# Half-width array tiles for PV, the state term and k^T v, in one burst for two chunks, in a fused linear-attention and ELU-MLP kernel

## The chip, the cores and the metric

The kernel runs on one core of a Trainium2 chip. The metric is device time in microseconds (us); smaller is better. Seven runs of the kernel before gave a median of 221.62 us, from 220.46 to 222.16.

## What is computed

Two stages follow each other. The first is causal linear attention with a decay per head, for batch 4, 8 heads, 768 tokens and head size 64. The reference works through the sequence in blocks and carries a 64x64 state per batch and head:

```python
intra = np.einsum('bhic,bhjc->bhij', qb, kb) * Dmask[None]
intra = np.einsum('bhij,bhjd->bhid', intra, vb)
inter = np.einsum('bhid,bhde->bhie', qb * lam_pow[None], kv_state)
out[:, :, sl] = intra + inter
kv_state = lam_block * kv_state + np.einsum('bhsd,bhse->bhde', kb_dec, vb)
```

The second takes the attention output as 3072 tokens of 512 features, multiplies by `w_in` (512x2048), applies ELU, and multiplies by `w_out` (2048x512). Inputs and output are float32; the kernel computes with float16 operands and float32 accumulation.

## The kernel before

The kernel uses blocks of 128 tokens. A chunk g is one block of one batch: g = 4 * block + batch, so there are 24 chunks, and chunk g needs the state that chunk g - 4 left. Heads are handled in four pairs (hp), two heads (hh) to a pair. For a chunk the steps are, with the letters of the kernel's own program:

- T (lines 272 to 300): q and k are transposed. Chunks 0 to 7 do it on TensorE, with DVE (line 298) scaling q while it copies and ACT (line 299) copying k. Chunks 8 to 23 use transposing DMAs on SP's queue.
- S (line 302): k q^T, 8 matmuls with 64 contracted rows, the two heads of a pair on the upper and lower half of the array. E (line 315) multiplies by the decay mask on DVE and makes `pp`.
- P (line 324): for each head pair two PV matmuls and, from chunk 4 on, one state-term matmul, all accumulated in one 128x128 block of the PSUM tile psO. So that one head's product fills only its own half, v lies in a tile `vz` with 64 zero columns between heads: head 0 takes [v0, 0], head 1 takes [0, v1] as 128-column weights. Then psO is copied to `xt`, the input of the MLP, by ACT (line 349, chunks 0 to 7) or by DVE with q's scale (line 351).
- U (line 374): k^T v for the state, 4 matmuls of 128x128 (line 381), of which only the two diagonal 64x64 blocks are used; DVE adds them into the state (line 392) after POOL has decayed the old one (`stt`, line 364). POOL also makes the decayed k, `kd` (line 175).
- 1 (line 418, matmuls on line 427): 8 or 16 matmuls by `w_in` into psH, of which there are two buffers; ACT does exp and relu (lines 433 and 434). `flush` at the next unit does the ELU combination `g` on DVE (line 410). Chunks 0 to 3 go singly, later ones in pairs with 256 columns.
- 2 (line 439, matmuls on line 449): four matmuls of 512 columns by `w_out` into psM, and after the fourth such unit of a chunk a copy (line 464) and a store.

The order is written out by hand. `OPEN` (line 51) lists the units of roughly the first 82 us in the order in which every engine's queue gets them; a number with colons is an MLP unit (1:chunk:part or 2:chunk:part). After it a loop (lines 530 to 557) puts the attention steps of each later pair of chunks at fixed places ahead of the pair's first MLP unit (`AT`, line 61): S 8 units ahead, P 5 and 4, U 3 and 2. `TAGS` names the PSUM bank of each product, eight banks in all. `POOL_ORDER` (line 45) is the order of POOL's queue: loads that convert to float16 on the way (q, k, v with a chunk number; i and o for parts of `w_in` and `w_out`), the index constants (iota), `kd` (d) and `stt` (m). An m waits for a token M in `OPEN`. Two tiles don't come over POOL: `RAW` (line 49) loads q of chunk 0 on SP's queue and k of chunk 0 on ACT's queue as float32, and DVE and ACT convert them (lines 128 and 130).

The zero columns are written once: DVE sets those of chunks 0 to 2 at the start (line 201), ACT those of chunk 3 (line 203) and those of the four pair buffers (line 468). The state tiles, which are block-diagonal, are zeroed too: one of each batch by DVE (line 206), the other by ACT (line 471).

Of the kernel before, what the change touches and what calls it, by code (L numbers as in the profile page):

```python
# [15 lines left out]
def kernel(  # L16
# [11 lines left out]
    nc = tc.nc  # L28
# [17 lines left out]
        "k2 v1 q2 iota q1 k1 i1 v0 i0 o1 v2 i3 o0 i2 q3 o2 k3 d0 d2 i4 d1 i5 o3 o7 v3 o5 o4 d3 "  # L46
        "i6 i7 o6 k4 q4 k10 k6 d4 v4 v8 q6 d5 q10 m4 v10 m5 m6 v6 d6 k8 q8 d7 m7"
    )
    RAW = "q0 k0"
    FIRST = "q0:0 c0 k0:1 c1 c2"  # L50
    OPEN = (
        "v3:1 Z2 Z0 z2 Z1 V0 z0 T0 z3 z1 V1 T1 S0 T2 S1 P0 S2 P1 1:0:0 P2 U0 1:1:0 1:2:0 2:0:0 "
        "1:0:1 2:1:0 M 1:1:1 T3 2:2:0 1:2:1 1:0:2 S3 2:1:1 1:1:2 2:2:1 2:0:1 P3 1:2:2 1:3:1 "
        "2:1:2 U1 1:3:0 2:0:2 1:1:3 Z3 U2 2:2:2 1:0:3 1:2:3 T5 2:1:3 M T4 2:0:3 2:2:3 1:3:2 "
        "S4:5 2:3:0 1:3:3 P4 E5 V3 2:3:1 U4 2:3:2 P5 U5 1:4:1 2:3:3 U3 M 1:4:0 W8 M W9 T6 "
        "1:4:2 T7 1:4:7 V2 S6:7 1:4:3 2:4:0 1:4:4 E7 2:4:1 1:4:5 P6 1:4:6 U7 P7 U6 2:4:2 1:6:0 "
        "1:6:1 2:4:3 S8:9 1:6:2 2:5:2 1:6:4 W10 2:5:1 W11 2:5:3 E9 1:6:3 2:6:0 2:5:0 U8 P8 "
        "1:6:5 1:6:6 2:6:1 P9 U9 1:6:7 2:6:2"
    )
    LAGU = 7  # L60
    AT = {"W": -13, "T": -9, "S": -8, "P": -5, "U": -3}
    TAGS = {
        "S0": "M0 M1", "S1": "C D", "S2": "A B", "S3": "A B",
        "P0": "H", "P1": "M0", "P2": "C", "P3": "A",
        "U0": "A", "U1": "A", "U2": "A", "U3": "B",
        "T0": "A B", "T1": "H H", "T2": "A B", "T3": "D", "T4": "A", "T5": "B", "T6": "A", "T7": "C",
        "T8": "B", "T9": "D", "M2": "C", "M3": "M0", "M4": "M1", "M5": "M0",
    }

# [17 lines left out]
    PB = 4  # L87
    vz1 = [cpool.tile([128, 1, 2 * H, 64], FP16, name=f"vz1_{i}") for i in range(4)]
    vz2 = [cpool.tile([128, 2, 2 * H, 64], FP16, name=f"vz2_{i}") for i in range(PB)]
# [6 lines left out]
    def emit_load(w, g0):  # L96
        n = size_of[g0]
        c, b = divmod(g0, B)
        x = {"q": q, "k": k, "v": v}[w]
        src = x[b : b + n, :, c * L : (c + 1) * L].rearrange("b h p d -> p (b h) d")  # L100
        if w == "v":
            t = vz1[g0] if n == 1 else vz2[(g0 - 4) // 2 % PB]
            assert g0 < 4 + 2 * PB or {f"{w}{g0 - i}" for w in "PU" for i in (7, 8)} <= seen
            vg[g0] = t
            dst = t[:, :, 0::2, :]
        else:
            t = asb.tile([128, n, H, 64], FP16, tag=f"{w}n{n}", name=f"{w}n{g0}", bufs=4)
            (qg if w == "q" else kg)[g0] = t
            dst = t[:]
        nc.gpsimd.dma_start(out=dst.rearrange("p b h d -> p (b h) d"), in_=src)  # L110
# [88 lines left out]
    def zero_v1(i, eng=0):  # L199
        if eng == 0:  # L200
            nc.vector.memset(vz1[i][:, :, 1::2, :], 0.0)
        else:
            nc.scalar.memzero(vz1[i][:, :, 1::2, :])

# [4 lines left out]
    for i in range(3):  # L209
        zero_v1(i)  # L210
# [52 lines left out]
    def default_tags(g):  # L263
        a, b = ("A", "B") if g % 2 == 0 else ("C", "D")
        for w, t in (("S", f"{a} {b}"), ("P", a), ("U", b), ("M", f"M{(g + 1) % 2}")):
            TAGS.setdefault(f"{w}{g}", t)
# [47 lines left out]

    def att_E(g):
        pts = psS.pop(g)
        for hh in range(2):
            P = asb.tile([128, NHP, 128], FP16, tag="pp", name=f"pp{g}_{hh}", bufs=6)
            nc.vector.tensor_tensor(  # L319
                out=P[:], in0=pts[hh][:], in1=mask[:, hh::2, :], op=ALU.mult  # L320
            )
            Pt[(g, hh)] = P

    def att_P(g):
        cb, b = divmod(g, B)
        vt = of(vg, g)
        qt, _ = qkT[g]
        po = bank(f"P{g}", 0, [128, NHP, 128], FP32, f"psO{g}")
        for hp in range(NHP):
            for hh in range(2):  # L330
                b0 = 4 * hp + hh
                nc.tensor.matmul(  # L332
                    po[:, hp, :], lhsT=vt[:, b0 : b0 + 2, :], rhs=Pt[(g, hh)][:, hp, :],
                    start=(hh == 0), stop=(hh == 1 and cb == 0), skip_group_check=True,
                )
            if cb > 0:
                nc.tensor.matmul(  # L337
                    po[:, hp, :], lhsT=st[b][cb % 2][:, hp, :], rhs=qt[:, hp, :],
                    start=False, stop=True, skip_group_check=True,
                )  # L340
        g0 = GFIRST[g]
        n = GSIZE[g0]
        if g0 not in xg:
            xg[g0] = asb.tile(
                [128, NHP, n * 128], FP16, tag=f"xt{n}", name=f"xt{g0}", bufs=4 if n == 1 else 2
            )
        dst = xg[g0][:, :, (g - g0) * 128 : (g - g0 + 1) * 128]
        if g < GPE:
            nc.scalar.copy(out=dst, in_=po[:])
        else:  # L350
            nc.vector.tensor_tensor(out=dst, in0=po[:], in1=qs[:], op=ALU.mult)  # L351
# [3 lines left out]
    def att_M(g):  # L355
        cb, b = divmod(g, B)
        if cb == NCB - 1:
            return
        assert f"U{g - B}" in seen
        old = st[b][cb % 2]  # L360
        for hh in range(2):
            r = slice(hh * 64, (hh + 1) * 64)
            tmp = asb.tile([128, NHP, 64], FP32, tag="stt", name=f"stt{g}_{hh}", bufs=8)
            nc.gpsimd.tensor_tensor(  # L364
                out=tmp[r], in0=old[r, :, r],
                in1=upp[r].unsqueeze(2).broadcast_to([64, NHP, 64]), op=ALU.mult,
            )
            stt[(g, hh)] = tmp
# [5 lines left out]
    def att_U(g):  # L374
        cb, b = divmod(g, B)
        if cb == NCB - 1:
            return
        vt = of(vg, g)
        pu = bank(f"U{g}", 0, [128, NHP, 128], FP32, f"psU{g}")
        for hp in range(NHP):  # L380
            nc.tensor.matmul(  # L381
                pu[:, hp, :].rearrange("p (h e) -> p h e", h=2),
                lhsT=kds[g][:, 2 * hp : 2 * hp + 2, :],
                rhs=vt[:, 4 * hp : 4 * hp + 3 : 2, :], start=True, stop=True,
            )
        new = st[b][(cb + 1) % 2]
        for hh in range(2):
            r = slice(hh * 64, (hh + 1) * 64)
            if cb == 0:
                nc.vector.tensor_copy(new[r, :, r], pu[r, :, r])  # L390
            else:
                nc.vector.tensor_tensor(  # L392
                    out=new[r, :, r], in0=stt.pop((g, hh))[r], in1=pu[r, :, r], op=ALU.add
                )

# [9 lines left out]
    def flush():  # L405
        while pending:
# [7 lines left out]
            for f in range(FB // n):  # L414
                for c in range(n):
                    gts[(g0 + c, j * (FB // n) + f)] = g[:, f, c, :]

    def mm1(g0, j):
# [3 lines left out]
        assert {f"P{g0 + i}" for i in range(n)} <= seen  # L422
        pH = ps.tile([128, FB * 128], FP32, tag="psH", bufs=2, name=f"psH{g0}_{j}")
# [43 lines left out]
    def zero_v(i):  # L467
        nc.scalar.memzero(vz2[i][:, :, 1::2, :])

# [12 lines left out]
    seen = {"v0", "v1", "v2"}  # L482

    def ready(t):

        if t[0] in "12M":
            return
        g = int(t[1:].split(":")[0])
        if t[0] == "P":
            assert (g < B or f"U{g - B}" in seen) and (  # L490
                (f"v{g}" if g < 3 else "v3" if g == 3 else f"V{(g - 4) // 2 % PB}") in seen
            )
# [4 lines left out]
        seen.add(t.split(":")[0])  # L497

    def run(t):
        ready(t)  # L500
        a = t[1:].replace(":", " ").split()
        a = [int(x) for x in a]
        if t[0] == "S":
            att_S(a[0])
            if len(a) == 1:
                att_E(a[0])
            else:
                att_S(a[1])
                att_E(a[0])
        else:  # L510
            {"T": att_T_pe, "E": att_E, "P": att_P, "U": att_U, "1": mm1, "2": mm2,
             "V": zero_v, "Z": zero_st, "v": zero_v1, "z": zero_st1,
             "q": lambda g, e: cast_raw(g, "q", e), "k": lambda g, e: cast_raw(g, "k", e),
             "c": lambda i: (emit_qs, emit_mask, emit_ks)[i](), "W": pool_work, "O": emit_stores, "M": lambda *a: next_M()}[t[0]](*a)
# [6 lines left out]
    done = set(prog)  # L521
# [8 lines left out]
    for g in range(0, NG, 2):  # L530
        u = place[(GFIRST[g], 0)] - (8 if GSIZE[GFIRST[g]] == 4 and g == GFIRST[g] else 0)
        for t, p in (
            (f"W{g}", AT["W"]), (f"W{g + 1}", AT["W"] + 2),
            (f"T{g}", AT["T"]), (f"T{g + 1}", AT["T"] + 1),
            (f"S{g}:{g + 1}", AT["S"]), (f"E{g + 1}", AT["S"] + 1),
            (f"P{g}", AT["P"]), (f"P{g + 1}", AT["P"] + 1),
            (f"U{g}", AT["U"]), (f"U{g + 1}", AT["U"] + 1),
        ):
            h = int(t[1:].split(":")[0])
            if t[0] == "W" and h < 8 or t[0] == "T" and h >= GPE:  # L540
                continue
            if t in done or f"{t[0]}{h}" in done or t[0] == "E" and f"S{h}" in done:
# [18 lines left out]
    for t in prog:  # L561
        run(t)
    emit_stores()
# [30 lines left out]
```

## Time and profile before

| | |
|---|---|
| median of 7 runs | 221.62 us |
| the profiled execution | 220.58 us |
| its span on the core, first to last instruction | 218.8 us |
| granted TensorE clock | 0.997 of full |
| PV matmuls (line 332) | 192 |
| state-term matmuls (line 337) | 80 |
| k^T v matmuls (line 381) | 80 |
| MLP matmuls (lines 427 and 449) | 896 and 388 |
| bytes moved by DMA | 24.70 MB |

The profiler records one execution. The page gives each engine's busy time and share of the span; a chain of work, followed back from the last instruction, with the share that each engine and line holds of it; and groups of instructions by line. PE is TensorE's matmuls and PEld its weight loads. The views by time say, for each stretch, what each engine did. Matmuls are pipelined, so the records of neighbours overlap, and the distance from start to start is the pace. In a timeline line the numbers are the start, the length from the first start to the last end, the engine, the line, the operation with output and inputs, the shapes (weights, then what streams) and how many are merged. In square brackets stands the time for which the engine was idle before, and what ended that.

The busiest groups outside TensorE are ACT's exp and relu (57.3 and 56.9 us, 597 and 593 ns each) and DVE's g (65.7 us, 685 ns each); pp takes 683 ns each on DVE, xt 691 on DVE and 589 on ACT.

### The profile page before, as it was taken

The page shows a single profiled execution, that of the slowest core. Times are in us where ns is not written, and L with a number is a line of the kernel's source. Part 1 is how long each engine was busy: PE and PEld are TensorE (multiplying, and loading weights), DVE is VectorE, ACT ScalarE, POOL GpSimd, SP SyncE. Part 2 cuts the span into 40 slices and gives each one's busy share as a digit, 9 for nine tenths or more (in the row PEclk, how much of TensorE's full clock was granted, in tenths as well). Part 3 has the DMA queues.
Part 4 walks back from the last instruction along what each step waited for, and adds up shares of the span by engine and source line. Part 5 has one row for each costly group of instructions (what it writes and reads, how often), then busy time and mean ns, then how long its engine had stood idle before and what let it go on. Part 6 is the DMA issues. An engine that isn't in the chain of part 4 may idle for free.

```text
span 218.8 us, 4793 instructions
## 1 busy us (share of the span) xinstructions
PE 203.6 (93%) x1892; PEld 144.6 (66%) x1892; DVE 130.7 (60%) x226; ACT 132.4 (61%) x251; POOL 95.5 (44%) x114
## 2 busy tenths in 40 slices
PE   0398999999999998999999999999999999999993
PEld 0277777777676676766766766766766767766641
DVE  3775457585886677567567567567567547434410
ACT  3846757865876456465466466466466476576630
POOL 7999880999975969259059054000000000000000
PEclk9999999999999999999999999999999999999998
DMA  5999999999998999969929929125128110111021
GB/s 104 165 188 189 196 196 172 156 201 170 145 126 157 156 193 146 167 39 182 142 23 176 143 20 174 48 63 84 49 64 83 48 51 1 51 49 43 5 85 62
DMA packets 101975, 24.70 MB, mean 113 GB/s; under 512 B 92608, under 2 KB 99008, under 8 KB 101952
## 3 DMA queue, kind: packets, MB, share of 16 engines
q0 software_dynamic: 78720, 13.37, 86.5%
q1 hardware_dynamic: 22192, 10.76, 24.6%
q10 hardware_dynamic: 1040, 0.26, 0.5%
q8 instruction: 15, 0.25, 0.4%
q14 instruction: 8, 0.07, 0.1%
HBM read 27.27 MB, written 6.29 MB: 153 GB/s over the span
## 4 chain that ended last, share of the span: by engine, by line
PE 89%; DMA 2%; DVE 2%; POOL 2%; ACT 2%; issue 1%; POOLq 0%; DVEq 0%; ACTq 0%
PE psM L449 38%; PE psH L427 37%; PE psO L332 5%; PE psS L310 3%; DMA kn<-in_k_dram 2%; PE psO L337 2%; PE psU L381 2%; PE psT L291 1%; DVE st L390 1%; POOL qn L110 1%; DVE g L410 1%; ACT e L433 1%; POOL kn L110 0%; ACT psH L434 0%; POOL vz L110 0%
## 5 line engine op out<-in xcount | busy, mean ns | idle before, releaser
L427 PE MATMUL psH<-xt,wi 128*128 128x256 f16 (+1 forms) x896 | 99.6, 258 | 2.4 <-DVE g L410 1.9
L433 ACT ACTIVATE e<-psH 128x512 f32<-128x512 f32 x96 | 57.3, 597 | 66.8 <-PE psH L427 65.4
L449 PE MATMUL psM<-wo,g 128*128 128x512 f16 (+1 forms) x388 | 97.0, 377 | 0.5 <-DVE osb L462 0.5
L410 DVE SCALAR_TENSOR_TENSOR g<-e,psH 128x512 f16<-128x512 f32 x96 | 65.7, 685 | 49.6 <-ACT psH L434 48.7
L427 PEld LDWEIGHTS <-wi 128*128 128x128 f16 x896 | 77.3, 98 | 27.2 <-DVE g L410 3.2
L434 ACT ACTIVATE psH<-psH 128x512 f32<-128x512 f32 x96 | 56.9, 593 | 0.0
L449 PEld LDWEIGHTS <-g 128*128 128x128 f16 x388 | 35.8, 98 | 27.6 <-issue 0.7
L319 DVE TENSOR_TENSOR pp<-psS,mask 128x512 f16<-128x512 f32 x48 | 30.7, 683 | 4.2 <-PE psS L310 4.2
L110 POOL DMA_DIRECT2D vz<-in_v_dram x14 | 15.4, 1098 | 25.0 <-PE psU L381 25.0
L175 POOL TENSOR_TENSOR kd<-kn,ks 128x512 f16<-128x512 f16 x20 | 20.9, 1047 | 6.5 <-DMA kn<-in_k_dram 5.5
L364 POOL TENSOR_TENSOR stt<-st,upp 64x256 f32<-64x256 f16 x32 | 19.5, 609 | 1.4
L332 PE MATMUL psO<-pp,vz 128*128 128x128 f16 x192 | 18.9, 226 | 0.0
L351 DVE TENSOR_TENSOR xt<-psO,qs 128x512 f16<-128x512 f32 x16 | 11.1, 691 | 11.7 <-PE psO L337 11.7
L464 ACT COPY osb<-psM 128x512 f32<-128x512 f32 (+1 forms) x24 | 13.8, 581 | 6.4 <-PE psM L449 6.4
L392 DVE TENSOR_TENSOR st<-stt,psU 64x256 f16<-64x256 f32 x32 | 13.4, 418 | 7.1 <-PE psU L381 6.5
L332 PEld LDWEIGHTS <-vz 128*128 128x128 f16 x192 | 15.6, 101 | 1.5 <-DMA vz<-in_v_dram 0.2
L110 POOL DMA_DIRECT2D qn<-in_q_dram x13 | 14.7, 1129 | 3.5 <-DMA kT<-kn 3.4
L110 POOL DMA_DIRECT2D kn<-in_k_dram x13 | 14.4, 1112 | 1.6 <-POOLq L578 0.8
L337 PE MATMUL psO<-qT,st 128*128 128x128 f16 x80 | 14.4, 219 | 0.0
L291 PE MATMUL psT<-ident,qn 128*128 128x128 f16 x32 | 3.8, 252 | 8.6 <-DVE qn L128 7.2
L310 PE MATMUL psS<-qT,kT 64*128 64x128 f16 x192 | 8.6, 228 | 0.1
L291 PEld LDWEIGHTS <-qn 128*128 128x128 f16 x32 | 2.5, 110 | 9.4 <-DVE qn L128 7.2
(40 smaller groups left out, 79.4 us busy)
## 6 DMA issues: line engine op xcount, KB each, us to landing
out_dram<-osb SPq DMA_DIRECT2D x23, 256.0 KB, 3.4
kn<-in_k_dram POOLq DMA_DIRECT2D x10, 256.0 KB, 7.2
qn<-in_q_dram POOLq DMA_DIRECT2D x10, 256.0 KB, 7.1
vz<-in_v_dram POOLq DMA_DIRECT2D x10, 256.0 KB, 7.7
wi<-in_moe_w_in_dram POOLq DMA_DIRECT2D x8, 256.0 KB, 7.4
wo<-in_moe_w_out_dram POOLq DMA_DIRECT2D x8, 256.0 KB, 8.3
vz<-in_v_dram POOLq DMA_DIRECT2D x4, 128.0 KB, 6.5
kn<-in_k_dram POOLq DMA_DIRECT2D x3, 128.0 KB, 6.2
```

The lines of the kernel that those rows point to most:

```text
L110: nc.gpsimd.dma_start(out=dst.rearrange("p b h d -> p (b h) d"), in_=src)
L175: nc.gpsimd.tensor_tensor(out=kd[:], in0=of(kg, g), in1=ks[:].unsqueeze(2).broadcast_to([128, H, 64]), op=ALU.mult,)
L310: nc.tensor.matmul(psS[g][hh][:, hp, :], lhsT=kt[r, hp, :], rhs=qt[r, hp, :], start=True, stop=True,)
L319: nc.vector.tensor_tensor(out=P[:], in0=pts[hh][:], in1=mask[:, hh::2, :], op=ALU.mult)
L332: nc.tensor.matmul(po[:, hp, :], lhsT=vt[:, b0 : b0 + 2, :], rhs=Pt[(g, hh)][:, hp, :], start=(hh == 0), stop=(hh == 1 and cb == 0), skip_ ...
L337: nc.tensor.matmul(po[:, hp, :], lhsT=st[b][cb % 2][:, hp, :], rhs=qt[:, hp, :], start=False, stop=True, skip_group_check=True,)
L364: nc.gpsimd.tensor_tensor(out=tmp[r], in0=old[r, :, r], in1=upp[r].unsqueeze(2).broadcast_to([64, NHP, 64]), op=ALU.mult,)
L410: nc.vector.scalar_tensor_tensor(out=g[:].rearrange("p f c t -> p (f c t)"), in0=e[:], scalar=-1.0, in1=r[:], op0=ALU.add, op1=ALU.min,)
L427: nc.tensor.matmul(pH[:, f * n * 128 : (f + 1) * n * 128], lhsT=wi16[i][:, kk, w * 128 : (w + 1) * 128], rhs=xg[g0][:, kk, :], start=(kk = ...
L433: nc.scalar.activation(e[:], pH[:], AF.Exp)
L434: nc.scalar.activation(pH[:], pH[:], AF.Relu)
L449: nc.tensor.matmul(psM[g][:, cols], lhsT=gts[(g, j * FB + f)], rhs=wo16[i][:, w, cols], start=first and f == 0, stop=end and f == FB - 1, ...
```

## The change

v is loaded into a plain tile without zero columns, and all zeroing of `vz` is gone. P writes each head of a pair by a matmul with 64 weight columns into its own 64 partitions of psO; the state term is split the same way, two matmuls of 64 weight columns for each pair of heads. A new token B runs P of two chunks and then U of both in one go; in it U has a matmul for each head, 64 weight columns by 64 streamed columns, into one shared PSUM tile. U of chunks 0 to 3 stays a full-width step of 4 matmuls by itself. From one chunk pair to the next there are 32 matmuls of P and 16 of U in a burst, for 24 and 8 before.

The copies out of PSUM (pp, xt, the state's update) no longer follow their matmuls at once on the queues: they are put on a list, `late`. Of S two are taken at once, of a burst the first, and every `flush` then takes one more behind its g. `until` takes more when a later step needs the result.

Only q of chunk 0 is still loaded as float32 on a hardware queue; k of chunk 0 is the first load on POOL's queue. `OPEN`, `POOL_ORDER` and the bank table are written anew.

```diff
-        "k2 v1 q2 iota q1 k1 i1 v0 i0 o1 v2 i3 o0 i2 q3 o2 k3 d0 d2 i4 d1 i5 o3 o7 v3 o5 o4 d3 "
-        "i6 i7 o6 k4 q4 k10 k6 d4 v4 v8 q6 d5 q10 m4 v10 m5 m6 v6 d6 k8 q8 d7 m7"
+        "k0 k1 iota q1 k2 v0 i0 v1 q2 i1 v2 o0 q3 i3 d0 i2 o1 k3 i4 o2 i5 o3 v3 d1 i7 d2 o4 m4 "
+        "o5 i6 d3 o7 o6 k4 q4 m5 v4 k10 q6 k6 q10 d4 d5 q8 d6 v6 m6 k8 v8 d7 v10 m7"
-    RAW = "q0 k0"
-    FIRST = "q0:0 c0 k0:1 c1 c2"
+    RAW = "q0"
+    FIRST = "q0:0 c0 c1 c2"
     OPEN = (
-        "v3:1 Z2 Z0 z2 Z1 V0 z0 T0 z3 z1 V1 T1 S0 T2 S1 P0 S2 P1 1:0:0 P2 U0 1:1:0 1:2:0 2:0:0 "
...
+        "z0 Z0 z3 z1 z2 Z2 Z1 T0 T1 S0 S1 P1 P0 T2 1:0:0 S2 1:1:0 U0 P2 M 1:2:0 1:0:1 2:0:0 "
...
+        "2:0:3 2:3:2 M 2:3:0 U3 B:P4:P5:U4:U5 W8 2:3:3 M 1:4:1 T6 W9 1:4:0 T7 2:3:1 1:4:3 S6:7 "
...
-    AT = {"W": -13, "T": -9, "S": -8, "P": -5, "U": -3}
+    AT = {"W": -13, "T": -9, "S": -8, "B": -4}
...
     def att_P(g):
...
+        R = [slice(0, 64), slice(64, 128)]
         for hp in range(NHP):
-            for hh in range(2):
-                b0 = 4 * hp + hh
+            for hh, r in enumerate(R):
                 nc.tensor.matmul(
-                    po[:, hp, :], lhsT=vt[:, b0 : b0 + 2, :], rhs=Pt[(g, hh)][:, hp, :],
-                    start=(hh == 0), stop=(hh == 1 and cb == 0), skip_group_check=True,
+                    po[r, hp, :], lhsT=vt[:, 2 * hp + hh, :], rhs=Pt[(g, hh)][:, hp, :],
+                    start=True, stop=(cb == 0), skip_group_check=True,
                 )
             if cb > 0:
-                nc.tensor.matmul(
-                    po[:, hp, :], lhsT=st[b][cb % 2][:, hp, :], rhs=qt[:, hp, :],
-                    start=False, stop=True, skip_group_check=True,
-                )
+                for r in R:
+                    nc.tensor.matmul(
+                        po[r, hp, :], lhsT=st[b][cb % 2][:, hp, r], rhs=qt[:, hp, :],
+                        start=False, stop=True, skip_group_check=True,
+                    )
...
+            for hp in range(NHP):
+                for hh in range(2):
+                    r = slice(hh * 64, (hh + 1) * 64)
+                    nc.tensor.matmul(
+                        pu[r, hp, :], lhsT=kds[g][:, 2 * hp + hh, :], rhs=vt[:, 2 * hp + hh, :],
+                        start=True, stop=True, skip_group_check=True,
+                    )
...
+    def burst(*ops):
+
+        us = [int(o[1:]) for o in ops if o[0] == "U" and int(o[1:]) // B < NCB - 1]
+        evs, i = [], 0
+        for o in ops:
+            if o[0] == "P":
+                evs += att_P(int(o[1:]))
+            elif int(o[1:]) in us:
+                if i == 0:
+                    pu = bank(o, 0, [128, 2, NHP, 64], FP32, f"psU{o[1:]}")
+                evs += att_U(int(o[1:]), pu[:, i])
+                i += 1
+        if evs:
+            late.insert(0, evs[0])
+            late.pop(0)()
+            late.extend(evs[1:])
...
     def flush():
...
+        if late:
+            late.pop(0)()
```

## The prediction, on record before the result

> **What bounds the kernel now.** I read the page's totals first, then its chain, then busy time by stage, then PE's timeline.
>
> ```profile
> span 218.8 us, 4793 instructions
> PE 203.6 (93%) x1892; PEld 144.6 (66%) x1892; DVE 130.7 (60%) x226; ACT 132.4 (61%) x251; POOL 95.5 (44%) x114
> ...
> PE 89%; DMA 2%; DVE 2%; POOL 2%; ACT 2%; issue 1%; POOLq 0%; DVEq 0%; ACTq 0%
> ```
>
> TensorE is 89% of the chain that ended last, and the next engines are at 61% and 60%. By stage (length, then busy us and count of PE, PEld, DVE, ACT, POOL):
>
> ```profile
> 0.00:15.50 15.50, 6.65 (x64) 4.85 (x65) 9.89 (x26) 8.38 (x20) 14.04 (x23) 1.00 1.48 150
> 15.50:82.00 66.50, 64.74 (x719) 48.35 (x718) 42.20 (x73) 44.84 (x85) 53.39 (x59) 1.00 2.01 172
> 82.00:208.00 126.00, 125.23 (x1079) 88.16 (x1078) 77.39 (x127) 77.15 (x143) 28.05 (x33) 1.00 0.68 80
> 208.00:219.00 11.00, 6.98 (x36) 3.29 (x34) 1.19 (x3) 2.04 (x4) 0.00 (x0) 0.92 0.20 73
> ```
>
> Three stages follow. Up to 15.5 us PE waits for loads and masks (POOL, which issues the loads, is busy 14.0 of 15.5). From 82 to 208 us PE never rests except 0.77, so what leaves PE there leaves the span. Between them PE is nearly full, with DMAs and POOL close behind. Now the price of each piece. Matmul records overlap, so I take the distance between starts, not the durations:
>
> ```profile
> 104.31 0.27 PE L332 MATMUL psO<-pp,vz 128*128 128x128 f16 x2
> 104.42 0.22 PE L337 MATMUL psO<-qT,st 128*128 128x128 f16 x1
> ...
> 104.98 1.03 PE L449 MATMUL psM<-wo,g 128*128 128x512 f16 x4
> ...
> 109.12 0.39 PE L381 MATMUL psU<-vz,kd 128*128 128x128 f16 x4
> 109.35 1.03 PE L449 MATMUL psM<-wo,g 128*128 128x512 f16 x4
> ...
> 113.91 1.04 PE L427 MATMUL psH<-xt,wi 128*128 128x256 f16 x8
> 114.88 0.62 PE L310 MATMUL psS<-qT,kT 64*128 64x128 f16 x16
> 115.43 1.04 PE L449 MATMUL psM<-wo,g 128*128 128x512 f16 x4
> ```
>
> PV plus state term of one chunk, 12 matmuls, take 104.98 - 104.31 = 0.67 us (56 ns each); k^T v, 4 matmuls, takes 0.23. The row-tiled S is the only tiled operation in this trace: eight L427 last 0.87, so S could start at 113.91 + 0.87 = 114.78; it starts at 114.88, and 16 matmuls take 0.55. A group of 8 S at 57.22 takes 0.33, so eight more cost 0.22: 27.6 ns each, half of 56, since two row tiles run at once. What remains, 0.55 - 0.45 = 0.10 behind and 0.10 ahead, is entering and leaving the tiled mode: 0.2 a burst.
>
> **What the Trainium skill says.** (1) "TensorEngine Tiling (Array Packing)", Key Properties: changing the tiling mode drains TensorE, and different tiles can load and multiply in parallel. The trace agrees for row tiles (0.10 each way, 27.6 ns). (2) The same page, Restrictions: column tiling switches Fast Weight Load off; "TensorE: Matmul & The Clock Gate", LDWEIGHTS, prices a load at columns/1.2 ns, 53 ns for 64 columns. No run here shows a column tile; full-width loads hide at 56 ns a matmul. (3) The clock-gate page, Part 3, The mechanism: weight loads overlap running matmuls "only when row_grp differs". Column tiles share all rows, so this speaks against the gain; yet the trace's full-array loads overlap anyway. (4) The same page, Measured speedup: three column tiles at 512 columns gave 2.38x. No run here shows it.
>
> **The change part by part.**
>
> *Bursts.* Of a pair of chunks, before: 2 x (0.67 + 0.23) = 1.80 us. After: 2 x 16 matmuls of 128 columns (PV 8, state 8) and 2 x 8 of 64 columns, all on half-width tiles, two at a time, in one excursion. At S's pace for all, 48 x 0.0276 + 0.2 = 1.53; saved 0.27. Eight pairs (chunks 4 to 19) save 2.2. Two pairs without k^T v: 2 x 0.67 = 1.34 becomes 32 x 0.0276 + 0.2 = 1.08, together 0.5 saved. Chunks 0 to 3 (8 PV each, alone or two together): 0.45 becomes 0.22 + 0.2, nothing. Sum: **-2.7**. Bounds: if 64-column matmuls go in half the time, 16 x 0.0138 less a burst, 1.8 more over eight bursts. From the other side, no overlap: 32 x 0.056 + 16 x 0.028 + 0.2 = 2.44 a pair, +0.64 x 8, +0.65 x 2 and +0.2 x 4, together +7.2. With loads of 53 ns one after another, 48 x 0.053 + 0.2 = 2.74, about +9.5. I take S's pace, as S too changes weights with every matmul. Break-even is (1.80 - 0.2)/48 = 33 ns.
>
> *Waits of the burst.* It stands one L427 group later than PV of the first chunk did (place -4 for -5) and 4 groups ahead of the first use of its xt, 4 x 1.73 = 6.9 us; L427 and L449 queue behind it on PE. In the trace S at 98.5 is followed by its PV at 104.3; the four pp products need 4 x 0.68 = 2.7 in DVE. DVE and ACT do the evacuations spread over later units; two xt of 0.69 fit in 6.9 us. Cost nothing; without that cover a late pp would cost 0.68. The 0.77 wait of L427 for g at 85.3, behind two pp on DVE, stays, since these come in the same order.
>
> *Zeros and casts.* Three v memsets on DVE (0.82 us at 0.86, idle then), ACT's five v zeros (0.40 and 4 x 0.63) and its cast of k0 (0.60) go. ACT is 61% busy and PE waits for none of them: nothing, save that kT of chunk 0 (ACT, 9.44) comes about 1 us earlier. But four state memsets of 0.27 now stand ahead of qT on DVE, two before.
>
> *Opening.* POOL's queue is now k0 k1 iota q1 k2 v0 i0 v1 q2 i1 v2 o0 q3 i3 kd0 i2 o1 k3. The first load was issued at 1.26 and landed 6.2 later; later 128 KB loads followed 0.5 to 0.9 apart, 256 KB weights about 1.3. So k0 lands near 7.3, k1 8.2, q1 8.9, k2 9.7, v0 10.6, i0 11.9, v1 12.7, q2 13.6, i1 14.9, v2 15.7, o0 17, q3 17.9, i3 19.2, i2 20.5, o1 21.8. Iota comes behind two issues, not three: 0.9 earlier. T0 is as before (7.3 against 7.24), since raw q still gates it. S0 follows qT0 (DVE: cast to 7.2, mask 1.2, memsets 1.1, qT 0.6), so about 10.1 for 11.03. But both S now precede PV: DVE does qT1 and four pp (3.3 us), PV at about 13.3, xt0 on ACT at 15.2; the first L427 at 15.3, before 15.51. Then S2, L427, k^T v, PV2, whose xt2 stands behind four exp/relu of 0.6 on ACT: third L427 group at about 19.5 (before 19.11), and the first L449 waits for o1 at 21.8, so the same work is done about **0.9 later** than before (21.77 to 22.7).
>
> *22 to 82 us.* Before had gaps of 0.6 (L427 at 50.6 for xt on ACT), 0.5 (55.7, for g), 0.3 (S6 and S7 apart, now together), 0.6 in smaller ones, about 2.0. The new order changes all these places; I let it keep 0.9, so **-1.1**. Here POOL's order has a new hook: stt of chunk 5 stands ahead of v4, k10, q6, k6, q10, kd4. It needs k^T v of chunk 1 (near 36.5 on PE), DVE's 0.87, then 1.3 itself, so v4 goes out near 38.7, as before (38.80), but k6 near 42.2 (before 31.2). With the median 7.2 it lands at 49.4; chunk 6 is transposed near 51 now (before 53.43). Covered by 1.6; without that cover each microsecond lands on PE.
>
> Sum: 220.58 (profiled execution; span 218.8 and 1.8 around it) - 2.7 + 0.9 - 1.1 = 217.7. That execution lies 1.04 under the median 221.62, so the median goes to **218.7**.
>
> **Rivals.** (A) Column tiles don't run two at a time: the array, or one path for weights without the fast load, takes them in turn. For it: skill points 2 and 3. Against: S's pace and point 4. It decides from 33 ns a matmul; at no overlap 221.6 + 7.2 - 0.2 = **228.6**, slower. (B) Tiles overlap but loads of 64 columns set about 33 ns: the change does not do what it says, and the rest cancels: **221.4**. (C) Tiles work, but the opening runs late: k6 lands 2 late, another gap stays where I gave 1.1 back: -2.7 + 0.9 + 2.5 is **222.3**. For it: POOL is busy 53 of 66 us there and the order is new; against: the 1.6 of cover.
>
> **How the numbers follow.** Forecast 0.60 (218.7, own range 216.9 to 220.6), A 0.13, B 0.13, C 0.14. About 0.3% (0.66 us) is what a measurement can tell from no change. Faster: all but 0.02 of the forecast, and a third of B and of C's lighter cases: 0.65. Same: 0.13. Slower: A, and half of C and a little of B: 0.22. The low end 216.5 takes in about the quick 64-column matmuls (218.7 - 1.8 = 216.9) with a little luck in the opening. The high end reaches over B and C to 223.5; A is left out with 0.13.
>
> **What would show it.** A burst of 1.5 us from the first PV to the next L449 or L427, 28 ns between starts; a burst of 2.4 is A, 1.8 is B. L427's first group near 15.3, first L449 near 21.8; a PE wait for kn at the transposes of chunk 6 is C. The forecast is wrong if bursts take over 1.8, or if PE's gaps between 15 and 82 us sum to more than they did.

## The result

The changed kernel takes a median of 224.94 us (12 runs, 222.29 to 228.44) against 221.18 us of the kernel before (31 runs, 220.46 to 222.35). The ratio is 1.0138, 95% interval 1.0114 to 1.0162: slower by 1.4%. Medians count every run, while ratios, here and below, leave out the runs that took over 1.5% more than the fastest of their kernel: here the two longest of the 12, which had the lowest TensorE clock (0.977). The forecast was 218.7 with a range from 216.5 to 223.5.

The profiled execution took 223.53 us. First the head of its page, PE's row of 40 slices, the granted clock, and the chain.

```profile
span 221.8 us, 5090 instructions
PE 201.2 (91%) x2036; PEld 139.1 (63%) x2036; DVE 130.1 (59%) x223; ACT 129.1 (58%) x245; POOL 96.5 (44%) x115
...
PE   0577999999997992999999999999999999999993
...
PEclk9999999999999999799999999999999999999999
...
PE 80%; DMA 11%; POOL 6%; SPq 1%; issue 0%; DVE 0%; ACT 0%; POOLq 0%
PE psM L487 36%; PE psH L465 35%; DMA kT<-kn 7%; DMA wo<-in_moe_w_out_dram 4%; PE psO L325 3%; PE psS L289 3%; PE psO L331 2%; POOL wi L136 1%; POOL kn L97 1%; POOL vn L97 1%; POOL qn L97 1%; PE psT L270 1%; PE psU L393 1%; SPq L255 1%; POOL kd L162 0%
```

PE is busy 2.4 us less than before, yet the span is 3.0 us longer. PE's share of the chain fell from 89% to 80%; 7% of it is a transfer that was not there, kT, k transposed by DMA. One slice of PE, near 86 us, is at 2, and the granted clock is at 7 tenths in the next. By stage, with the columns of the prediction's table:

```profile
50.00:82.00 32.00, 30.35 (x339) 21.59 (x334) 21.96 (x39) 20.35 (x40) 30.33 (x34) 1.00 2.10 159
82.00:208.00 126.00, 121.79 (x1155) 82.87 (x1153) 76.21 (x125) 75.32 (x141) 26.15 (x31) 0.99 0.66 85
```

In the stage where PE had rested 0.77 us it now rests 4.2.

**The bursts are better than forecast.** A burst in PE's timeline:

```profile
110.19 1.04 PE L465 MATMUL psH<-xt,wi 128*128 128x256 f16 x8
111.15 0.25 PE L325 MATMUL psO<-pp,vn 128*64 128x128 f16 x2
111.23 0.22 PE L331 MATMUL psO<-qT,st 128*64 128x128 f16 x2
...
112.07 0.42 PE L393 MATMUL psU<-vn,kd 128*64 128x64 f16 x16
112.42 1.04 PE L487 MATMUL psM<-wo,g 128*128 128x512 f16 x4
```

Eight L465 last 0.87, so the burst could start at 111.06 and starts at 111.15. The next unit starts at 112.42: 1.36 us in all, 1.80 before. The 32 matmuls of 128 columns give way to the next at 112.07, about 28 ns each. The 16 of 64 columns take 0.35 with leaving the mode; leaving costs 0.09 (worked out under y_split), so they are at 16 ns. The trace has the starts in pairs: the two tiles start 3 to 4 ns apart, and from pair to pair it is 56 ns with 128 columns and 32 with 64.

**The loss lies in two places.** PE's timeline at S of chunks 8 and 9, and of 10 and 11:

```profile
68.99 0.40 PE L289 MATMUL psS<-qT,kT 64*128 64x128 f16 x8
71.04 0.40 PE L289 MATMUL psS<-qT,kT 64*128 64x128 f16 x8 [1.65 <-DMA kT<-kn]
...
82.31 1.04 PE L465 MATMUL psH<-xt,wi 128*128 128x256 f16 x8
84.88 0.40 PE L289 MATMUL psS<-qT,kT 64*128 64x128 f16 x8 [1.53 <-DMA kT<-kn]
87.96 0.46 PE L289 MATMUL psS<-qT,kT 64*128 64x128 f16 x8 [2.68 <-DMA kT<-kn]
88.35 3.47 PE L465 MATMUL psH<-xt,wi 128*128 128x256 f16 x16
91.66 1.03 PE L487 MATMUL psM<-wo,g 128*128 128x512 f16 x4
```

Distances between starts, less what the same steps take without a wait: from S of 8 to S of 9 it is 2.05 for 0.22, 1.8 lost; L465 at 82.31 takes 2.57 for 0.97, 1.6 lost; from S of 10 to S of 11 it is 3.08 for 0.22, 2.9 lost; and the 16 L465 at 88.35 take 3.31 for 1.74, 1.6 lost at the lowered clock, which was 0.50 of full from 89 to 91 us. That is 7.9 us. The kernel before lost 0.95 near 84 us (1.82 for 0.87), which isn't seen here:

```profile
83.49 1.05 PE L427 MATMUL psH<-xt,wi 128*128 128x256 f16 x8
85.31 1.05 PE L427 MATMUL psH<-xt,wi 128*128 128x256 f16 x8 [0.77 <-DVE g L410]
```

**Where the waits come from.** SP's queue of the changed kernel, issue by issue:

```profile
54.03 1.34 SPq L255 DMA_TRANSPOSE qT<-qn  x1
59.08 1.19 SPq L255 DMA_TRANSPOSE kT<-kn  x1
60.31 0.66 SPq L437 DMA_DIRECT2D out_dram<-osb  x1
61.08 1.43 SPq L255 DMA_TRANSPOSE qT<-qn  x1
62.55 2.45 SPq L255 DMA_TRANSPOSE kT<-kn  x1
65.09 10.38 SPq L437 DMA_DIRECT2D out_dram<-osb  x3
75.65 1.80 SPq L255 DMA_TRANSPOSE qT<-qn  x1
77.54 1.22 SPq L255 DMA_TRANSPOSE kT<-kn  x1
78.86 1.28 SPq L255 DMA_TRANSPOSE qT<-qn  x1
80.20 1.40 SPq L255 DMA_TRANSPOSE kT<-kn  x1
```

The first kT waits until 59.08, because k8 was issued on POOL only at 54.13 and landed at 59.07. kT of chunk 9 goes out at 62.55 and lands 8.4 us later, at 71.0, where S of 9 stands. Then three stores hold the queue from 65.09 to 75.5: the last is of chunk 4 and waits for ACT to copy a product that PE makes at 73.1. Behind them stand the transposes of 10 and 11; the last goes out at 80.20 and lands 7.7 later, at 87.9. In the kernel before these four went out from 67.50 to 72.8, ahead of the stores of chunks 4 and 5. Its SP queue:

```profile
60.50 1.30 SPq L276 DMA_TRANSPOSE qT<-qn  x1
...
65.42 1.27 SPq L276 DMA_TRANSPOSE kT<-kn  x1
66.78 0.53 SPq L403 DMA_DIRECT2D out_dram<-osb  x1
67.50 1.22 SPq L276 DMA_TRANSPOSE qT<-qn  x1
...
71.51 1.29 SPq L276 DMA_TRANSPOSE kT<-kn  x1
72.89 4.10 SPq L403 DMA_DIRECT2D out_dram<-osb  x2
```

What holds k8 back in the changed kernel is in POOL's timeline:

```profile
30.43 1.17 POOL L97 DMA_DIRECT2D qn<-in_q_dram  x1
37.44 1.29 POOL L365 TENSOR_TENSOR stt<-st,upp 64x256 f32<-64x256 f16 x2 [5.84 <-DVE st L403]
38.68 1.21 POOL L97 DMA_DIRECT2D vn<-in_v_dram  x1
...
54.13 1.20 POOL L97 DMA_DIRECT2D kn<-in_k_dram  x1
```

stt of chunk 5 waits 5.84 us for a state; ten loads stand behind it, k8 among them.

For chunks 8 and 9 this is only half of the comparison with the kernel before. There k8 landed at 58.69, no more than 0.4 us sooner, and the four transposes went out later, from 60.50 to 65.42. But the last took 2.50 us, where it takes 8.45 in the changed kernel, and landed at 67.91, 0.7 ahead of S of 9 at 68.57. An earlier k8 can make up for such a long landing; what made it long is another question, which the experiments leave open.

**Theory:** the tiles gain some 4 us, and two hold-ups in the rewritten order cost twice that: stt on POOL's queue makes S of 8 and 9 wait, the store on SP's queue makes S of 10 and 11 wait. **Rivals:** the tiles themselves slow PE or pull its clock down; or the DMA engines are so full that no order helps.

### The profile page after: what moved, and what is told of

It is laid out like the page before. It is cut to its first block, busy times and chain, and to the rows that moved or that the text cites. A ratio compares the mean times of both kernels' runs of the same rounds, so it can differ in the third digit from the quotient of the medians.

```text
span 221.8 us, 5090 instructions
## 1 busy us (share of the span) xinstructions
PE 201.2 (91%) x2036; PEld 139.1 (63%) x2036; DVE 130.1 (59%) x223; ACT 129.1 (58%) x245; POOL 96.5 (44%) x115
## 4 chain that ended last, share of the span: by engine, by line
PE 80%; DMA 11%; POOL 6%; SPq 1%; issue 0%; DVE 0%; ACT 0%; POOLq 0%
PE psM L487 36%; PE psH L465 35%; DMA kT<-kn 7%; DMA wo<-in_moe_w_out_dram 4%; PE psO L325 3%; PE psS L289 3%; PE psO L331 2%; POOL wi L136 1%; POOL kn L97 1%; POOL vn L97 1%; POOL qn L97 1%; PE psT L270 1%; PE psU L393 1%; SPq L255 1%; POOL kd L162 0%
## 5 line engine op out<-in xcount | busy, mean ns | idle before, releaser
L465 PE MATMUL psH<-xt,wi 128*128 128x256 f16 (+1 forms) x896 | 101.3, 261 | 0.9 <-ACT xt L346 0.9
L465 PEld LDWEIGHTS <-wi 128*128 128x128 f16 x896 | 78.7, 100 | 26.6 <-DVE g L444 1.3
L487 PEld LDWEIGHTS <-g 128*128 128x128 f16 x388 | 36.4, 98 | 30.4 <-issue 1.8
L97 POOL DMA_DIRECT2D vn<-in_v_dram x14 | 15.5, 1106 | 20.7 <-PE psU L393 20.7
L365 POOL TENSOR_TENSOR stt<-st,upp 64x256 f32<-64x256 f16 x32 | 19.5, 610 | 10.3 <-DVE st L403 5.8
L97 POOL DMA_DIRECT2D kn<-in_k_dram x14 | 15.4, 1102 | 0.9 <-POOLq L621 0.8
L325 PE MATMUL psO<-pp,vn 128*64 128x128 f16 x192 | 12.4, 230 | 2.1 <-DMA vn<-in_v_dram 2.1
L325 PEld LDWEIGHTS <-vn 128*64 128x64 f16 x192 | 10.1, 114 | 5.0 <-DMA vn<-in_v_dram 2.4
L289 PEld LDWEIGHTS <-kT 64*128 64x128 f16 x192 | 5.8, 98 | 9.5 <-DMA kT<-kn 6.5
L331 PE MATMUL psO<-qT,st 128*64 128x128 f16 x160 | 10.0, 219 | 0.0
```

The lines of the kernel that those rows point to most:

```text
L97: nc.gpsimd.dma_start(out=t[:].rearrange("p b h d -> p (b h) d"), in_=src)
L289: nc.tensor.matmul(psS[g][hh][:, hp, :], lhsT=kt[r, hp, :], rhs=qt[r, hp, :], start=True, stop=True,)
L325: nc.tensor.matmul(po[r, hp, :], lhsT=vt[:, 2 * hp + hh, :], rhs=Pt[(g, hh)][:, hp, :], start=True, stop=(cb == 0), skip_group_check=True,)
L331: nc.tensor.matmul(po[r, hp, :], lhsT=st[b][cb % 2][:, hp, r], rhs=qt[:, hp, :], start=False, stop=True, skip_group_check=True,)
L365: nc.gpsimd.tensor_tensor(out=tmp[r], in0=old[r, :, r], in1=upp[r].unsqueeze(2).broadcast_to([64, NHP, 64]), op=ALU.mult,)
L465: nc.tensor.matmul(pH[:, f * n * 128 : (f + 1) * n * 128], lhsT=wi16[i][:, kk, w * 128 : (w + 1) * 128], rhs=xg[g0][:, kk, :], start=(kk = ...
```

## The experiments

Each run is compared with the kernel before on the same chip.

### x_full: full-width matmuls in the changed order

```diff
-                    po[r, hp, :], lhsT=vt[:, 2 * hp + hh, :], rhs=Pt[(g, hh)][:, hp, :],
-                    start=True, stop=(cb == 0), skip_group_check=True,
+                    po[:, hp, :], lhsT=vt[:, 2 * hp : 2 * hp + 2, :], rhs=Pt[(g, hh)][:, hp, :],
+                    start=(hh == 0), stop=(hh == 1 and cb == 0), skip_group_check=True,
...
-                evs += att_U(int(o[1:]), pu[:, i])
+                evs += att_U(int(o[1:]))
```

U of odd chunks also takes another PSUM bank. The kernel leaves out the separation of two heads, as the expectation says; the count and shapes of PE's matmuls are those of the kernel before.

> The changed kernel with its order, queues and loads kept, but PV, state term and k^T v as full-width matmuls again (2 + 1 per head pair and 4 per chunk; since v has no zero columns now, each PV product also fills the other head's half, so the output leaves the separation of the heads out). Theory (the half-width tiles gain, the transposing DMAs of chunks 8 to 11 lose): a burst goes from 1.27 + 0.1 us to about 1.80, so ten bursts cost +4 us, of which up to 1.5 is absorbed in the waits for kT near 69 and 85 us; total 226 to 229 us. Rival (the half-width tiles cause the loss, by their own pace or by pulling the TensorE clock down): 218 to 221 us, and no waits for kT.

227.5 us, ratio 1.0299 (1.0241 to 1.0357), 1.6% over that of the changed kernel. All three waits for kT are there (2.2, 1.5 and 2.2 us lost), and the slow L465 after them. So the waits and the lowered clock don't come from the half-width tiles, which help.

### x_m5, x_w10 and x_m5w10: the two hold-ups, one at a time and together

x_m5 is the change to `POOL_ORDER`, x_w10 the moves in `OPEN`, x_m5w10 both.

```diff
-        "o5 i6 d3 o7 o6 k4 q4 m5 v4 k10 q6 k6 q10 d4 d5 q8 d6 v6 m6 k8 v8 d7 v10 m7"
+        "o5 i6 d3 o7 o6 k4 q4 v4 k10 q6 k6 q10 m5 d4 d5 q8 d6 v6 m6 k8 v8 d7 v10 m7"
...
-... B:P6:P7:U6:U7 1:4:7 1:6:1 2:5:2 ... 2:6:1 W10 W11 1:6:7 2:6:2
+... B:P6:P7:U6:U7 1:4:7 W10 1:6:1 W11 2:5:2 ... 2:6:1 1:6:7 2:6:2
```

> The changed kernel with one step of POOL's queue moved: the decayed state of chunk 5 (stt) goes behind the loads of v4, k10, q6, k6 and q10. Theory: POOL no longer holds these loads back for 5.8 us, all later loads come about 3 us earlier, kT of chunk 9 lands before S needs it, and S of chunks 8 and 9 loses its wait of 1.8 us; the wait of S for chunks 10 and 11 (about 4.5 us with the clock drop) shrinks only by what the earlier part gives, since the transposes stand behind a store on SP. 220 to 223 us. Rival (the loss comes from SP's order alone): S of 8 and 9 still waits, 224 us.

221.66 us, ratio 1.0012 (0.9994 to 1.0031), in the range of the theory. kT of chunk 9 goes out at 60.20 and lands at 68.3, and S of 8 and 9 has no wait. PE's timeline:

```profile
69.20 1.03 PE L487 MATMUL psM<-wo,g 128*128 128x512 f16 x4
70.16 0.62 PE L289 MATMUL psS<-qT,kT 64*128 64x128 f16 x16
70.71 1.92 PE L465 MATMUL psH<-xt,wi 128*128 128x256 f16 x16
```

That of 10 and 11 stays: the transposes are still issued from 74.99 on, and 1.3 and 1.8 us are lost.

> The changed kernel with the pool work of chunks 10 and 11 (their four transposing DMAs, and the loads of chunk 14 and 15) called about 10 units earlier, so that on SP's queue they stand ahead of the stores of chunks 3 and 4 and not behind. Theory: the transposes of 10 and 11 are issued near 66 us and not from 75.65 on, S of 10 and 11 doesn't wait (saves 1.6 + 2.9 us) and the TensorE clock keeps full (saves another 1.3); S of 8 and 9 still waits about 1.8 or more. 217 to 220 us. Rival (DMA bandwidth, not the order of SP's queue, sets when they land): the wait moves with the data, 223 us or more.

220.76 us, ratio 0.9949 (0.9923 to 0.9975): the median of all runs is just over the range of the theory. The transposes of chunks 10 and 11 go out from 65.94 on, and their S has no wait. But S of 8 and 9 waits longer (2.8 us lost, and 1.4 in the matmuls after it, at a clock of 0.50).

> Both of the moves: stt of chunk 5 behind the five loads, and the pool work of chunks 10 and 11 earlier. Theory (two independent hold-ups, one on POOL's queue and one on SP's): both waits for kT go, PE is dense from 25 to 208 us, 214.5 to 217.5 us, under the kernel before by some 2%. Rival (bandwidth): the transposes land no earlier than in the first move alone, 220 us or more.

216.86 us, ratio 0.9814 (0.9788 to 0.984), as the theory has it. By the ratios, x_m5 saves 2.8 us against the changed kernel, x_w10 4.2 and both 7.2: the two savings add up. SP's queue:

```profile
56.44 1.20 SPq L255 DMA_TRANSPOSE kT<-kn  x1
57.69 0.82 SPq L437 DMA_DIRECT2D out_dram<-osb  x1
58.61 1.80 SPq L255 DMA_TRANSPOSE qT<-qn  x1
60.45 1.79 SPq L255 DMA_TRANSPOSE kT<-kn  x1
62.34 0.55 SPq L437 DMA_DIRECT2D out_dram<-osb  x1
63.07 2.00 SPq L255 DMA_TRANSPOSE qT<-qn  x1
65.16 1.22 SPq L255 DMA_TRANSPOSE kT<-kn  x1
66.49 1.51 SPq L255 DMA_TRANSPOSE qT<-qn  x1
68.09 1.55 SPq L255 DMA_TRANSPOSE kT<-kn  x1
69.73 4.34 SPq L437 DMA_DIRECT2D out_dram<-osb  x3
```

The transposes take as long from issue to landing as in the changed kernel (6.9 to 8.4 us); they are issued earlier. kT of chunk 9, at 60.45, lands near 68.5, and S of 9 starts at 69.12: 0.6 to spare. The rival that no order helps falls. It does not follow that the DMA engines have no part in it, since the landings stayed as long.

### y_full: what the tiles are worth without the hold-ups

The edit of x_full on x_m5w10.

> The kernel with both hold-ups removed (stt of chunk 5 behind the five loads, pool work of chunks 10 and 11 earlier), but PV, state term and k^T v as full-width matmuls in the same bursts (the separation of the two heads of a pair is left out of the output, as in the first full-width run). Theory: with no waits for kT left to absorb anything, it costs what the tiles save: ten bursts, 8 x 0.44 + 2 x 0.24 = 4.0 us, and about 0.5 in the opening; 220.5 to 222 us against 216.9, level with the kernel before. Rival (the tiles are worth little, and the gain of the two moves comes from the new order): under 218.5 us.

220.91 us, ratio 0.9999 (0.9983 to 1.0016). A burst takes 1.79 us, and 1.36 in x_m5w10. Against 216.86 the tiles are worth 4.05 us; the kernel before took 220.94 beside this run and 220.96 beside the other, so the two can be compared. The new order, freed of the hold-ups but with full-width matmuls, is level with the kernel before: apart from the tiles, the change brings nothing.

### y_sp: only the transposes moved

x_m5w10, with D10 and D11 for the moved W10 and W11.

```diff
-... 1:4:7 1:6:1 2:5:2 ...
+... 1:4:7 D10 1:6:1 D11 2:5:2 ...
...
-        if g >= GPE:
+        if g >= GPE and g not in qkT:
             att_T_dma(g)
...
-... "W": pool_work,
+... "W": pool_work, "D": att_T_dma,
```

> As the kernel with both hold-ups removed, but of the pool work of chunks 10 and 11 only the four transposing DMAs on SP's queue are called earlier; their loads (chunks 14 and 15), kd and stt stay where the changed kernel has them. Theory (a store that stands ahead on SP's queue holds the transposes back): 216.5 to 217.5 us, as with all of it moved. Rival (it was the earlier loads or POOL's products): the wait of S for chunks 10 and 11 is back, 220 us or more.

217.4 us, ratio 0.9829 (0.98 to 0.9859): 0.5 more than x_m5w10, which the intervals don't tell apart. The place on SP's queue is what counts, not the loads and products of POOL that x_w10 also moved.

### z_k8w10: one load first, the hold-up left in

The edit goes on top of x_w10.

```diff
-... d4 d5 q8 d6 v6 m6 k8 v8 d7 v10 m7
+... d4 d5 q8 k8 d6 v6 m6 v8 d7 v10 m7
```

> The changed kernel with the pool work of chunks 10 and 11 earlier, stt of chunk 5 left where it holds up POOL, and only the load k8 moved ahead of kd6, v6 and stt6 on POOL's queue. Theory (what counts is when k8 lands, since all four transposes of 8 and 9 are queued behind it): k8 goes out near 47.7 us and not at 54.1, its first transpose near 54 and not at 59, S of 8 and 9 doesn't wait, 216.5 to 218 us. Rival (the hole in the loads before 38.7 us is what can't be made good, whichever load is put first): S of 8 and 9 still waits a microsecond or more, or PV of chunk 6 waits for v6, 219 us or more.

216.78 us, ratio 0.9788 (0.9743 to 0.9832). stt still waits 6.12 us on POOL, but k8 goes out at 48.78. The transposes of 8 start at 56.37, later than expected, yet the last of 9 goes out at 61.23, and S of 9 loses 0.4 us, for 2.8 in x_w10. Of this 2.4, kT of 9 landing sooner (70.65 for 72.02) accounts for 1.4; the rest is that PE reached S 1.0 later in this execution, the longest of the four (218.07). The times show what the trace shows in part: 1.6% less than x_w10 by the ratios, and level with x_m5w10. So the hole in the loads before 38.7 can be made good; what hurt was that k8 stood so far behind it.

### y_split: the price of one more excursion

x_m5w10, with each burst from chunk 10 on cut in two. An excursion is one entering and leaving of the tiled mode.

```diff
-            (f"S{g}:{g + 1}", AT["S"]), (f"B:P{g}:P{g + 1}:U{g}:U{g + 1}", AT["B"]),
+            (f"S{g}:{g + 1}", AT["S"]), (f"B:P{g}:U{g}", AT["B"] - 1), (f"B:P{g + 1}:U{g + 1}", AT["B"]),
...
-... ("U", "C"), ...
+... ("U", "CD"[g % 2]), ...
```

> The kernel with both hold-ups removed, but from chunk 10 on each pair's burst is cut in two, one for each chunk, with a unit of other work between; the matmuls are the same. Theory (entering and leaving the half-width mode costs 0.2 us): seven more excursions, +1.4 us, 218.3 us (217.8 to 218.8). Rival (the switch hides behind other work when it is not repeated for S): no more than +0.4.

218.83 us, ratio 0.9902 (0.9878 to 0.9927): 1.97 us more than x_m5w10, just over the range. Half a burst in PE's timeline:

```profile
86.01 1.04 PE L465 MATMUL psH<-xt,wi 128*128 128x256 f16 x8
...
86.98 0.25 PE L325 MATMUL psO<-pp,vn 128*64 128x128 f16 x2
...
87.45 0.29 PE L393 MATMUL psU<-vn,kd 128*64 128x64 f16 x8
87.67 1.04 PE L487 MATMUL psM<-wo,g 128*128 128x512 f16 x4
```

Entering takes 0.10 (86.98 against 86.01 + 0.87 = 86.88). The eight 64-column matmuls and leaving take 0.22, the 16 of a whole burst 0.35: eight cost 0.13, or 16 ns each, and 0.09 is left for leaving. An excursion is 0.19, seven are 1.3 us. S of 9 lost 0.5 in this execution, before the first cut burst, which the edit should not touch. The remaining 0.2 isn't explained.

### y_k0hw and z_best

y_k0hw puts k of chunk 0 back on ACT's hardware queue. z_best does too, and takes 2:6:2 off the end of OPEN.

```diff
-    RAW = "q0"
-    FIRST = "q0:0 c0 c1 c2"
+    RAW = "q0 k0"
+    FIRST = "q0:0 c0 k0:1 c1 c2"
...
-        "k0 k1 iota q1 k2 v0 i0 ...
+        "k1 iota q1 k2 v0 i0 ...
...
-        "... 1:6:7 2:6:2"
+        "... 1:6:7"
```

> The kernel with both hold-ups removed, and k of chunk 0 as float32 on ACT's hardware queue with a conversion on ACT again, so that only its place in the load order is undone. Theory: in the changed kernel T of chunk 0 starts at 5.6 us (7.24 before) since raw q lands earlier with half the traffic beside it, and the first product by w_in at 14.1 (15.5 before); undoing it makes T later by 1.6 but takes 128 KB out of POOL's queue ahead of v0 and i1, which set the first product; 216.5 to 218 us, within 1 us of 216.9. Rival (the early start of T is worth its 1.6 us): 218.5 us or more.

216.51 us, ratio 0.9802 (0.9769 to 0.9836), the same as x_m5w10. T of chunk 0 is back at 7.27 us and the first product by w_in at 15.02 (14.25 in x_m5w10), and nothing of that is left at the end.

> The version that the runs point to: both hold-ups removed, k of chunk 0 on ACT's hardware queue again, and the unit 2:6:2 taken out of the hand-written list, so that the loop puts a product by w_out between the two products by w_in that follow S of chunks 10 and 11. Theory: the wait of 0.95 us for g near 83 us goes, 215.5 to 216.3 us. Rival (the wait only moves to the next pair of units): 216.5 us as without it.

216.09 us, ratio 0.9768 (0.9734 to 0.9802): 2.3% faster than the kernel before. The wait for g shrank from 0.95 to some 0.6 but moved to the first product after S; the gain on 216.51 is within the intervals.

## Why the prediction was wrong

*What bounds the kernel* was right and still misled. That PE was never idle after 82 us told what a gain on PE is worth as long as the feeds keep up. It said nothing about how little slack they had: in the kernel before kT of chunk 9 landed 0.7 us ahead of its use, in x_m5w10 0.6.

*The bursts* were right in sign and mechanism. -2.7 was forecast, 4.05 came (x_m5w10 against y_full). Mis-sized was the 64-column matmul, taken at S's 28 ns and in fact 16; that is near the lower bound given. Point (1) of the Trainium skill, "TensorEngine Tiling (Array Packing)", Key Properties, holds for column tiles too: a drain of 0.09 to 0.10 us each way, and two tiles at a time. Points (2) and (3), on the lost fast load and on loads overlapping only across row groups ("TensorE: Matmul & The Clock Gate", The mechanism), did not bite: every matmul had a load of its own, the pace was 28 and 16 ns a matmul, and in U a tile took new weights every 32 ns, where point (2) prices a load at 53. No run shows whether the fast load was off. Rivals A and B are refuted.

*The opening* was right in its sum. T started at 5.61 and not at 7.3; with raw k back on its queue (y_k0hw) it started at 7.27. The first product by w_in came at 14.12 (forecast 15.3), the third group at 19.27 (19.5), and PE then waited for o1 until 22.46 (21.8). What the kernel before had done at 23.97, and one more group of 0.89, was done at 25.98: 1.1 later, for the 0.9 of the forecast.

*22 to 82 us* holds the first part of the step that failed: the path from POOL's loads over SP's queue to S. The forecast has 1.1 us of gain there, with "Here POOL's order has a new hook ... Covered by 1.6". The gain came: the gaps of 0.6, 0.5 and 0.3 that it names are gone, and by the distances between starts PE loses 1.3 us less than before from 25 to 68 us. The hook was there as described, v4 out at 38.68 and k6 at 42.14. But the prediction followed it to one of the loads behind it, k6, and stopped. k8 was issued at 54.13, and behind k8 stand three of the four transposes of chunks 8 and 9. The last landed 8.4 us after its issue, and S of 9 had no cover for that: 1.8 us. So the second sign of being wrong came: PE's idle time between 15.5 and 82 us rose from 1.8 to 3.4 us.

*SP's queue was not priced at all*, the larger part of the failed step. The transposes of 10 and 11 had been moved in the program's order from ahead of the stores of chunks 4 and 5 to behind that of chunk 4. The order of the built program's SP instructions shows it without a run:

```
before: store 3, qT10, kT10, qT11, kT11, store 4, store 5
after:  store 0, store 3, store 4, qT10, kT10, qT11, kT11, store 5
```

A store waits for ACT's copy, and the copy for PE's last product. From 82 us on this cost 6.1 us (1.6, 2.9 and 1.6), where the forecast kept one wait of 0.77. The wait at S of 9 adds little: without it (x_m5) these transposes go out only 0.7 us sooner. "The 0.77 wait ... stays" was right in itself: in x_m5w10 L465 at 83.72 waits 0.77 for g again. In the changed kernel the longer waits covered it.

*The sum.* 220.58 - 4.0 (bursts, 8 x 0.44 + 2 x 0.24) + 1.1 (opening) - 1.3 (gaps from 25 to 68 us) + 7.9 (kT and clock) - 0.95 (the covered wait for g) is 223.3, and the execution took 223.53. Without the last two terms it is 216.4, and x_m5w10's execution took 216.57. So of the forecast's three terms two came near their size and the bursts better; what it lacked is the 7.9, for waits that it had put at nothing. Rival C named the right kind of trouble, late loads in the new order, at the wrong place (PE did not wait for k6) and a third of the size.

*What stays open* is why the transposes of 8 and 9 took so much longer to land than in the kernel before, though issued earlier.

## What to carry to other kernels

When an order is rewritten, list each DMA-issuing queue instruction by instruction, before and after, and follow every transfer behind a moved wait to its last consumer, not only to the first. A store that waits for a result doesn't belong ahead of a transpose that the engine making the result needs soon after: here that cost 4.2 us. A part that gains and a part that loses can be bound up in one change: undoing each alone told them apart, and turned a loss of 1.4% into a gain of 2%.

## What the runs showed of the hardware

- On half-width column tiles, a matmul of 128 streamed columns cost 28 ns and one of 64 columns 16 ns, each with its own weight load. Two tiles started 3 to 4 ns apart.
- Entering and leaving the tiled mode cost 0.09 to 0.10 us each.
- In the changed kernel PE was idle for 1.53 and 2.68 us with 8 matmuls between, and the next 16 L465 took 3.31 us and not 1.74, at a granted clock of 0.50. In x_w10 one idle time of 2.64 us was followed by the same clock and 1.4 us lost. But after 1.65 us alone (S of 9 in the changed kernel), after 2.01 alone (the same in x_full), and after 1.21 and 1.62 with 8 matmuls between (x_m5), the clock stayed full. So some waits for kT cost more than their length; where the line lies these runs don't tell.
- The SBUF transposes by DMA took 2.4 to 7.6 us from issue to landing for chunks 8 to 11 in the kernel before, and 4.3 to 8.7 in the changed one. The two quickest, 2.50 and 2.44, were issued at 65.42 and 67.50 in the kernel before, where the loads had landed by 65.99 and the next was issued at 68.23. In the changed kernel loads were in flight up to 74.0. That the loads are the cause was not tested.
